# A softmax moved to ScalarE head by head, in a kernel of chunked attention and two MLPs

## The chip, the cores and the metric

The kernel runs on one core of one Trainium2 chip. The metric is the device time of one execution in microseconds. TensorE does the matmuls and some transposes, ScalarE activations and copies, VectorE elementwise work, reductions and 32x32 transposes. SyncE's queue issues nearly all DMAs.

## The reference

Three stages follow one another: attention in chunks, a first pair of layers with an ELU between them, and a second pair with a scaled square of a ReLU.

```python
B, H, S, D = 4, 8, 768, 64;  n_mem = 8;  chunk, left, right = 32, 16, 8
for each chunk c of 32 queries:
    keys = the 8 memory keys, then those from c_start-16 to c_end+8, cut at 0 and S
    scores = q_c @ keys.T / sqrt(D)
    a = exp(scores - max(scores));  a = a / (sum(a) + 1e-9)
    out_c = a @ values
x = out of all heads, as (3072, 512)
h = x @ w_in;   g = where(h > 0, h, exp(min(h, 0)) - 1);  x = g @ w_out      # (512, 2048), (2048, 512)
h = x @ w_in2;  g = s * max(h, 0)**2 + b;                 out = g @ w_out2
```

Every chunk has 64 keys (8 + 16 + 32 + 8); in the first chunk of a batch the 16 to its left don't exist, in the last the 8 to its right. Their scores are masked.

## The kernel before

Attention is cut into 24 units of 128 queries (four chunks) with all 8 heads, six units for each batch; `j` is a unit's place in its batch. A unit goes through three steps. S (`scores`, L213, and `softmax`, L223): 64 small matmuls put the scores of a unit into two PSUM banks, one for each half of the heads, 4 heads of 64 columns in each; then comes the softmax of 8 heads of 64 columns in 128 rows: a mask is added (only in units whose `j` is 0 or 5), the maximum of each head is reduced and subtracted, one ACTIVATE takes the exponential of the whole block, and VectorE sums each head, adds 1e-9, takes the reciprocal and multiplies. P (`step_P`, L245): the block is transposed, for units 0 to 5 on TensorE with a copy to `pt` by `hi_copy` (L174), for later ones by 16 VectorE transposes (L258). V (`values`, L270, and `to_x`, L282): 64 small matmuls with the values, and copies out. From unit 6 on the V step of a unit and the S step of the next share their PSUM tile (`step_VS`, L315).

The tile for scores, of two banks, has one buffer (`ps_a`), so the scores of a unit wait until the softmax of the unit before has read its own for the last time.

The order: units 0, 1 and 2 are worked off before the first h matmul, with the scores of units 3 and 4 (the loop at L506), beside the conversion of the first weights (`split_w`: two ScalarE steps, L131 and L132, two VectorE steps, L135 and L138, a ScalarE copy, L149, and a VectorE subtraction, L184). Then the first layer pair runs in chunks of 128 hidden features for 8 tiles of 384 tokens. Each chunk has 12 matmuls for h (`h1`, L346), a chain of ScalarE and VectorE for the ELU and its split into two parts (L350, L351, L352, L180, L184), and 12 matmuls into four accumulators (`out1`, L386), which come two chunks later. Six chunks of tile 0, all of tile 1, the rest of tile 0 and tiles 2 to 4 have steps of the remaining units between them (`beside`, L512); tiles 0 and 1 also convert weights. From tile 5 on the second pair's weights are prepared. The second pair (`first_layer`, `second_layer`) has seven products for each block; its last copies (L734 on VectorE, L736 on ScalarE) take the two accumulators of the last product, and `put` (L688) stores each with one DMA on SyncE's queue.

The framework's planner orders the instructions of each engine by priority, dependence and its own estimate of durations. On the chip each engine then works off its queue in that order. Loads of k, q, v and weights are all in SyncE's one queue, in order; k, q and v have two buffers, so the load of `v` for a unit waits for the values matmuls of the unit two before it.

Of the kernel before, what the change touches and what calls it, by code (L numbers as in the profile page):

```python
# [8 lines left out]
F32 = mybir.dt.float32  # L9
# [3 lines left out]
AF = mybir.ActivationFunctionType  # L13
ALU = mybir.AluOpType
AX = mybir.AxisListType
# [3 lines left out]
B, H, S, D, NMEM = 4, 8, 768, 64, 8  # L19
CH, LEFT, RIGHT = 32, 16, 8  # L20
# [3 lines left out]
U = 4 * CH  # L24
NKEY = LEFT + U + RIGHT + NMEM
UPB = S // U
NU = B * UPB
NP = H // 2
NU0 = 6
# [4 lines left out]
HN, NT2 = 512, 3  # L34
# [3 lines left out]
NC, NCK = U // CH, LEFT + CH + RIGHT + NMEM  # L38
# [15 lines left out]
def tile_attention_then_two_mlps(ctx, tc, q_in, k_in, v_in, w1, w2, s_in, b_in, out):  # L54
# [17 lines left out]
    nc = tc.nc  # L72
    SCALE = 1.0 / float(D) ** 0.5
    NEG = -1.0e30
# [14 lines left out]
    const = ctx.enter_context(tc.tile_pool(name="const", bufs=1))  # L89
# [19 lines left out]
    part_dram = dp.tile([P, KT, MAXN], F32, name="part1")  # L109

    ident = const.tile([P, P], F32, name="ident")
    cmasks = [const.tile([U, NCK], F32, name=f"cmask{i}") for i in range(2)]
    s_sb = const.tile([P, 1], F32, name="s_sb")
    b_sb = const.tile([P, 1], F32, name="b_sb")

# [46 lines left out]
    op = [actx.enter_context(tc.tile_pool(name="op", bufs=3))]  # L162
# [20 lines left out]
    def sub(lo, src, hi):  # L183
        return nc.vector.tensor_tensor(out=lo, in0=src, in1=f(hi), op=ALU.subtract)  # L184
# [12 lines left out]

    def set_up():

        for m in cmasks:  # L200
            nc.vector.memset(m, 0.0)
        nc.vector.memset(cmasks[0][:CH, NMEM:NMEM + LEFT], NEG)
        nc.vector.memset(cmasks[1][U - CH:, NCK - RIGHT:], NEG)
        make_identity(nc, ident)

    def own_keys(u):

        return sms[u % 2].rearrange("p r z n -> p z r n")

    def by_halves(a):  # L210
        return a.rearrange("p (z r) -> p z r", z=2).unsqueeze(3).to_broadcast([U, 2, NP, NCK])
# [11 lines left out]
    def softmax(u, ps):  # L223
        src = ps[:, :, :NP * NCK].rearrange("p z (r n) -> p z r n", r=NP)
        sm, j = own_keys(u), u % UPB
        if j in (0, UPB - 1):
            mask = cmasks[j > 0].unsqueeze(1).unsqueeze(1).to_broadcast([U, 2, NP, NCK])
            nc.vector.tensor_tensor(out=sm, in0=src, in1=mask, op=ALU.add)
            src = sm
        nmx, sums, rs = (ap2.tile([U, H], F32, tag=nm, name=nm) for nm in ("nmx", "sums", "rs"))  # L230
        nc.vector.tensor_reduce(out=nmx.rearrange("p (z r) -> p z r", z=2), in_=src, op=ALU.max, axis=AX.X)
        nc.vector.tensor_tensor(out=sm, in0=src, in1=by_halves(nmx), op=ALU.subtract)
        nc.scalar.activation(out=sm, in_=sm, func=AF.Exp, scale=SCALE)
        nc.vector.tensor_reduce(out=sums.rearrange("p (z r) -> p z r", z=2), in_=sm, op=ALU.add, axis=AX.X)
        nc.vector.tensor_scalar(out=rs, in0=sums, scalar1=1e-9, scalar2=None, op0=ALU.add)
        nc.vector.reciprocal(out=rs, in_=rs)
        nc.vector.tensor_tensor(out=sm, in0=sm, in1=by_halves(rs), op=ALU.mult)

    def step_S(u):

        ps = two_banks("S")
        scores(u, ps)
        softmax(u, ps)
# [71 lines left out]
    def step_VS(u):  # L315

        ps = two_banks("VS")
        values(u, ps)
        last = scores(u + 1, ps)
        to_x(u, ps, last)  # L320
        softmax(u + 1, ps)


    def mm3(o, a, b, sa, sb, first, last, again=False):

        nc.tensor.matmul(o, sa(a[0]), sb(b[0]), start=first, stop=False, skip_group_check=again)  # L326
        nc.tensor.matmul(o, sa(a[0]), sb(b[1]), start=False, stop=False, skip_group_check=again)  # L327
        return nc.tensor.matmul(o, sa(a[1]), sb(b[0]), start=False, stop=last, skip_group_check=again)  # L328
# [133 lines left out]

    warm(6, pt.rearrange("p h n -> p (h n)")[:, :2 * U])
    set_up()

    nload = [1, 0]
# [67 lines left out]
    def next_piece(layer, i, j):  # L534

        load_pieces(used[0] + 11)
        assert pieces[used[0]] == (layer, i, j)
        used[0] += 1
        return ws[used[0] - 1]
# [102 lines left out]
    def bank(nm):  # L642
        return psp.tile([P, HN], F32, tag="b", name=nm)

    def add(o, x, y):
        return nc.vector.tensor_tensor(out=o, in0=x, in1=y, op=ALU.add)

    def sub2(o, x, y):
        return nc.vector.tensor_tensor(out=o, in0=x, in1=y, op=ALU.subtract)

    def aside(ps, nm):
        o = evp.tile([P, HN], F32, tag="ev", name=nm)
        nc.scalar.activation(out=o, in_=ps, func=AF.Copy)  # L653
        return o
# [30 lines left out]
            sub2(g[:, 1], g[:, 2], g[:, 1])  # L685
            add(g[:, 1], g[:, 1], g[:, 0])

    def put(o, t, m, z):  # L688
        t0 = (2 * t + z) * HN
        nc.sync.dma_start(out=out[:, m, t0:t0 + HN], in_=o)  # L690

    def second_layer(t, gs, beside):

        keep, acc = {}, {}
        for j in ORDER:
            block = {1: 0, 2: 3, 6: 1, 5: 1, 7: 0, 3: 2, 4: 3}[j]
            if j in (1, 2, 5):
                acc[j] = [bank("psL") for _ in range(2)]
            o = acc[BANK[j]]
            for q, g in enumerate(gs):  # L700
                gh, gl = (ghp.tile([P, 2, HN], F32R, tag=nm, name=nm) for nm in ("g2h", "g2l"))
                nc.scalar.activation(out=gh, in_=g[:, block], func=AF.Copy)  # L702
                sub(gl, g[:, block], gh)
                if j == 1:
                    sub2(g[:, 0], g[:, 1], g[:, 0])
                elif j == 2:
                    sub2(g[:, 3], g[:, 3], g[:, 1])
                elif j == 6:
                    sub2(g[:, 1], g[:, 2], g[:, 1])
                for ii in range(2):  # L710
                    w = next_piece(1, 2 * q + ii, j)
                    for m in range(2):
                        mm3(o[m], (w[:, 0], w[:, 1]), (gh[:, ii], gl[:, ii]), lambda a: a[:, m * P:(m + 1) * P],
                            lambda a: a, j in (1, 2, 5) and q == ii == 0, q == 3 and ii == 1,
                            j not in (1, 2, 5))
                if j in (5, 7, 3):
                    next(beside, None)
            for m in range(2):
                if j in (1, 6, 5):
                    keep[j, m] = aside(o[m], "keep")  # L720
                    continue
                r = outp.tile([P, HN], F32, tag="r", name="r")
                if j == 2:
                    add(r, keep[1, m], o[m])
                    put(r, t, m, 0)
                elif j == 7:
                    add(r, keep[5, m], o[m])
                    put(r, t, 2 + m, 1)
                elif j == 3:
                    add(r, keep[6, m], o[m])  # L730
                    put(r, t, m, 1)
                else:
                    if m:
                        nc.vector.tensor_copy(r, o[m])  # L734
                    else:
                        nc.scalar.activation(out=r, in_=o[m], func=AF.Copy)  # L736
                    put(r, t, 2 + m, 0)

    assert next(p2["blocks"], None) is None
    for t in range(NT2):  # L740
        gs = [g2p.tile([P, 4, 2, HN], F32, tag="g", name="g2") for _ in range(NF // 4)]
        for i in range(NF // 2):
            first_layer(t, i, gs[i // 2])
        steps2 = load_blocks(t + 1) if t + 1 < NT2 else iter(())
        second_layer(t, gs, steps2)
        assert next(steps2, None) is None
# [55 lines left out]
```

## Time and profile before

| what | us |
|---|---|
| median of 3 runs | 1099.0 (1098.36 to 1099.37) |
| the profiled execution | 1097.48 |
| its span, first to last instruction | 1095.7 |
| TensorE busy | 1076.3 |
| VectorE busy | 783.9 |
| ScalarE busy | 591.9 |

A busy time is a sum over instructions, with matmuls pipelined. The granted clock is the share of TensorE's full 2.4 GHz that the throttle let through; over the span it is 0.992.

### The profile page before, as it was taken

The numbers are of one execution on the slowest core, as the hardware profiler recorded it, in microseconds if no ns is written. First come the engines' busy times: TensorE is split into PE (matmuls) and PEld (weight loads), VectorE is DVE, ScalarE is ACT, GpSimd is POOL, SyncE is SP. The second block draws the span as 40 slices with busy tenths as digits, with TensorE's granted clock in tenths as the row PEclk, the third lists the DMA queues.
The fourth block names the chain that finished last, engine by engine and source line by source line (L and its number), as shares of the span: only waits on it lengthen the run. The fifth ranks groups of instructions, "written<-read, shape, count | busy, mean of one in ns | idle before, by whom it ended". The sixth has DMA issues, their size and how long they took to land.

```text
span 1095.7 us, 20629 instructions
## 1 busy us (share of the span) xinstructions
PE 1076.3 (98%) x8206; PEld 964.4 (88%) x8206; DVE 783.9 (72%) x1299; ACT 591.9 (54%) x939; POOL 0.7 (0%) x6
## 2 busy tenths in 40 slices
PE   7999999999999999999999999999999999999998
PEld 5889999999999999999999987788888788888886
DVE  6899856777777777898884656796266695375844
ACT  4888534344344346887875455644355653355542
POOL 0000000000000000000000000000000000000000
PEclk7999999999999999999999999999999999999999
DMA  8965032442433316888876366777767777776773
GB/s 305 377 223 214 1 109 94 146 144 93 142 117 121 114 40 206 328 329 303 328 289 253 90 192 190 240 211 224 229 192 196 222 207 226 207 193 192 205 190 124
DMA packets 98113, 213.70 MB, mean 195 GB/s; under 512 B 9952, under 2 KB 27360, under 8 KB 95968
## 3 DMA queue, kind: packets, MB, share of 16 engines
q1 hardware_dynamic: 97440, 211.59, 60.3%
q8 instruction: 65, 1.06, 0.4%
q10 hardware_dynamic: 576, 0.79, 0.2%
q14 instruction: 32, 0.26, 0.1%
HBM read 164.89 MB, written 47.45 MB: 194 GB/s over the span
## 4 chain that ended last, share of the span: by engine, by line
PE 87%; DVE 6%; DMA 4%; ACT 3%; issue 1%; SPq 0%; ACTq 0%; DVEq 0%
PE psH L326 14%; PE psH L328 14%; PE psH L327 14%; PE psL L327 7%; PE psL L328 7%; PE acc L326 7%; PE psL L326 7%; PE acc L327 7%; PE acc L328 7%; DVE pt L258 2%; DMA xc<-y_dram 1%; PE psVS L278 1%; DMA xl<-x_dram 1%; PE psVS L219 1%; PE psV L278 1%
## 5 line engine op out<-in xcount | busy, mean ns | idle before, releaser
L326 PE MATMUL psH<-xh,w 128*128 128x384 f32 x512 | 174.9, 342 | 2.4 <-ACT pt L180 1.0
L326 PE MATMUL acc<-gh,w 128*128 128x384 f32 x512 | 172.7, 338 | 1.3 <-DVE big L380 0.8
L328 PE MATMUL psH<-xh,w 128*128 128x384 f32 x512 | 173.0, 338 | 0.0
L327 PE MATMUL psH<-xl,w 128*128 128x384 f32 x512 | 172.6, 337 | 0.2 <-DVE xl L184 0.2
L328 PE MATMUL acc<-gh,w 128*128 128x384 f32 x512 | 171.8, 336 | 0.0
L327 PE MATMUL acc<-gl,w 128*128 128x384 f32 x512 | 171.7, 335 | 0.0
L702 ACT ACTIVATE g2h<-g 128x1024 fp32r<-128x1024 f32 x84 | 88.9, 1058 | 95.6 <-PE psL L328 95.5
L327 PE MATMUL psL<-g2l,ws 128*128 128x512 f32 x336 | 133.0, 396 | 1.4 <-DVE g2l L184 1.4
L184 DVE TENSOR_TENSOR g2l<-g,g2h 128x1024 fp32r<-128x1024 f32 x84 | 102.3, 1222 | 44.3 <-ACT g2h L702 44.0
L328 PE MATMUL psL<-g2h,ws 128*128 128x512 f32 x336 | 132.9, 395 | 0.0
L326 PE MATMUL psL<-g2h,ws 128*128 128x512 f32 x336 | 132.5, 396 | 0.1
L326 PE MATMUL psH<-xc,ws 128*128 128x512 f32 x336 | 131.7, 397 | 0.5 <-ACT p L653 0.5
L327 PE MATMUL psH<-xc,ws 128*128 128x512 f32 x336 | 131.0, 390 | 0.0
L328 PE MATMUL psH<-xc,ws 128*128 128x512 f32 x336 | 131.0, 390 | 0.0
L350 ACT ACTIVATE g<-psH 128x384 f32<-128x384 f32 x128 | 62.5, 488 | 111.9 <-PE psH L328 65.3
L180 ACT ACTIVATE gh<-g 128x384 fp32r<-128x384 f32 x128 | 67.0, 523 | 88.0 <-DVE g L352 86.9
L352 DVE SCALAR_TENSOR_TENSOR g<-g,psH 128x384 f32<-128x384 f32 x128 | 70.4, 550 | 47.8 <-ACT g L351 46.9
L326 PEld LDWEIGHTS psH<-xh,w 128*128 128x128 f32 x512 | 96.7, 189 | 5.1 <-ACT pt L180 1.2
L326 PEld LDWEIGHTS acc<-gh,w 128*128 128x128 f32 x512 | 96.1, 188 | 2.8 <-DVE big L380 1.1
L327 PEld LDWEIGHTS psH<-xl,w 128*128 128x128 f32 x512 | 96.7, 189 | 0.5 <-DVE xl L184 0.4
L328 PEld LDWEIGHTS psH<-xh,w 128*128 128x128 f32 x512 | 96.7, 189 | 0.2
L327 PEld LDWEIGHTS acc<-gl,w 128*128 128x128 f32 x512 | 96.2, 188 | 0.1
(97 smaller groups left out, 1667.9 us busy)
## 6 DMA issues: line engine op xcount, KB each, us to landing
ws<-s_dram SPq DMA_DIRECT2D x336, 256.0 KB, 3.0
raw<-w SPq DMA_DIRECT2D x64, 512.0 KB, 5.5
s_dram<-right SPq DMA_DIRECT2D x16, 1024.0 KB, 4.6
kb<-k SPq DMA_DIRECT2D x24, 512.0 KB, 5.5
v<-v SPq DMA_DIRECT2D x24, 512.0 KB, 4.1
s_dram<-left SPq DMA_DIRECT2D x16, 768.0 KB, 3.6
q<-q SPq DMA_DIRECT2D x24, 256.0 KB, 5.4
out<-r SPq DMA_DIRECT2D x24, 256.0 KB, 3.5
```

Source lines behind the costliest of these rows:

```text
L180: return nc.scalar.activation(out=hi, in_=src, func=AF.Copy)
L184: return nc.vector.tensor_tensor(out=lo, in0=src, in1=f(hi), op=ALU.subtract)
L219: mm = nc.tensor.matmul(ps[o, z, r * NCK:(r + 1) * NCK], q[rows, r * U + c * CH:r * U + (c + 1) * CH], kb[rows, r, c * NCK:(c + 1) * NCK], ...
L258: nc.vector.transpose(out=pt[k * CH:(k + 1) * CH, :, rows], in_=sm[rows, :, z, n0:n0 + CH])
L278: nc.tensor.matmul(ps[r % 2 * D:(r % 2 + 1) * D, z, o:o + CH], v[rows, (r * NC + c) * D:(r * NC + c + 1) * D], pt[rows, r, cs], start=True ...
L326: nc.tensor.matmul(o, sa(a[0]), sb(b[0]), start=first, stop=False, skip_group_check=again)
L327: nc.tensor.matmul(o, sa(a[0]), sb(b[1]), start=False, stop=False, skip_group_check=again)
L328: return nc.tensor.matmul(o, sa(a[1]), sb(b[0]), start=False, stop=last, skip_group_check=again)
L350: nc.scalar.activation(out=g[:, :n], in_=ps[:, :n], func=AF.Relu, scale=-1.0)
L352: nc.vector.scalar_tensor_tensor(out=g[:, :n], in0=g[:, :n], scalar=-1.0, in1=ps[:, :n], op0=ALU.add, op1=ALU.max)
L702: nc.scalar.activation(out=gh, in_=g[:, block], func=AF.Copy)
```

## The change

The softmax has two forms. Units 3 to 5 keep the old one. All others take the exponential head by head: the maximum is scaled by -1/sqrt(D) and given to ScalarE as a bias, which reads the scores in PSUM, writes the exponentials to SBUF and gives the sum of the head as a second output. For masked units of either form the mask is no longer added: VectorE writes -1e30 over the masked scores in PSUM, and the mask tiles and their four memsets at the start go. The last copy of the program is halved: VectorE copies the left half of the columns and ScalarE the right, and each half has its own store, one on SyncE's queue and one on ScalarE's.

```diff
-    cmasks = [const.tile([U, NCK], F32, name=f"cmask{i}") for i in range(2)]
...
     def set_up():
-        for m in cmasks:
-            nc.vector.memset(m, 0.0)
-        nc.vector.memset(cmasks[0][:CH, NMEM:NMEM + LEFT], NEG)
-        nc.vector.memset(cmasks[1][U - CH:, NCK - RIGHT:], NEG)
         make_identity(nc, ident)
...
     def softmax(u, ps):
         src = ps[:, :, :NP * NCK].rearrange("p z (r n) -> p z r n", r=NP)
         sm, j = own_keys(u), u % UPB
-        if j in (0, UPB - 1):
-            mask = cmasks[j > 0].unsqueeze(1).unsqueeze(1).to_broadcast([U, 2, NP, NCK])
-            nc.vector.tensor_tensor(out=sm, in0=src, in1=mask, op=ALU.add)
-            src = sm
+        if j == 0:
+            nc.vector.memset(src[:CH, :, :, NMEM:NMEM + LEFT], NEG)
+        elif j == UPB - 1:
+            nc.vector.memset(src[U - CH:, :, :, NCK - RIGHT:], NEG)
...
-        nc.vector.tensor_tensor(out=sm, in0=src, in1=by_halves(nmx), op=ALU.subtract)
-        nc.scalar.activation(out=sm, in_=sm, func=AF.Exp, scale=SCALE)
-        nc.vector.tensor_reduce(out=sums.rearrange("p (z r) -> p z r", z=2), in_=sm, op=ALU.add, axis=AX.X)
+        if 3 <= u < NU0:
+            nc.vector.tensor_tensor(out=sm, in0=src, in1=by_halves(nmx), op=ALU.subtract)
+            nc.scalar.activation(out=sm, in_=sm, func=AF.Exp, scale=SCALE)
+            nc.vector.tensor_reduce(out=sums.rearrange("p (z r) -> p z r", z=2), in_=sm, op=ALU.add, axis=AX.X)
+        else:
+            nc.vector.tensor_scalar(out=nmx, in0=nmx, scalar1=-SCALE, scalar2=None, op0=ALU.mult)
+            for h in range(H):
+                z, r = divmod(h, NP)
+                nc.scalar.activation(out=sm[:, z, r], in_=src[:, z, r], func=AF.Exp, scale=SCALE,
+                                     bias=nmx[:, h:h + 1], accum_out=sums[:, h:h + 1])
...
-    def put(o, t, m, z):
+    def put(o, t, m, z, dma=nc.sync, cols=slice(0, HN)):
         t0 = (2 * t + z) * HN
-        nc.sync.dma_start(out=out[:, m, t0:t0 + HN], in_=o)
+        dma.dma_start(out=out[:, m, t0 + cols.start:t0 + cols.stop], in_=o[:, cols])
...
+                    if m and t == NT2 - 1:
+                        a, b = slice(0, HN // 2), slice(HN // 2, HN)
+                        nc.vector.tensor_copy(r[:, a], o[m][:, a])
+                        nc.scalar.activation(out=r[:, b], in_=o[m][:, b], func=AF.Copy)
+                        put(r, t, 2 + m, 0, nc.sync, a)
+                        put(r, t, 2 + m, 0, nc.scalar, b)
+                        continue
```

## Rows read from the trace of the kernel before

**Rows 1.** The page's chain that ended last: shares of the span by engine.
```profile
PE 87%; DVE 6%; DMA 4%; ACT 3%; issue 1%; SPq 0%; ACTq 0%; DVEq 0%
```

**Rows 2.** Windows: stretch, its length, busy us of each engine, PEclk, DMA share, GB/s.
```profile
8.00:16.00 8.00, 4.46 (x140) 3.19 (x140) 7.29 (x16) 3.84 (x7) 0.00 (x0) 0.99 1.00 389
16.00:33.00 17.00, 15.42 (x344) 13.32 (x344) 12.71 (x24) 9.37 (x17) 0.00 (x0) 0.50 0.86 318
...
56.00:64.00 8.00, 7.92 (x100) 6.89 (x99) 7.92 (x17) 6.84 (x15) 0.00 (x0) 1.00 0.93 375
64.00:76.00 12.00, 9.97 (x121) 8.72 (x119) 11.60 (x28) 11.12 (x22) 0.00 (x0) 1.00 0.19 56
...
130.00:390.00 260.00, 257.49 (x3217) 250.63 (x3216) 185.12 (x441) 107.54 (x203) 0.00 (x0) 1.00 0.36 117
```

**Rows 3.** Timeline, 6 to 27 us: start, length, engine, line, what, [idle before <-releaser].
```profile
6.24 0.86 PE L219 MATMUL psS<-kb,q 64*32 64x64 f32 x64
7.14 0.69 DVE L228 TENSOR_TENSOR sm<-psS,cmask 128x512 f32<-128x512 f32 x1 [5.42 <-PE psS L219]
8.92 0.86 PE L219 MATMUL psS<-kb,q 64*32 64x64 f32 x64
10.13 0.61 ACT L233 ACTIVATE sm<-sm 128x512 f32<-128x512 f32 x1
13.94 0.69 DVE L237 TENSOR_TENSOR sm<-sm,rs 128x512 f32<-128x512 f32 x1
15.15 0.68 ACT L131 ACTIVATE raw<-raw 128x512 f32<-128x512 f32 x1 [0.40 <-DMA raw<-w]
16.28 0.57 ACT L180 ACTIVATE pt<-psP 128x512 f32<-128x512 f32 x1
16.91 1.93 PE L278 MATMUL psV<-pt,v 64*64 64x32 f32 x64 [0.20 <-ACT pt L180]
22.79 1.11 PE L251 MATMUL psP<-ident,sm 128*128 128x128 f32 x4
24.65 1.72 PE L278 MATMUL psV<-pt,v 64*64 64x32 f32 x56 [0.75 <-ACT pt L180]
```

**Rows 4.** Waits of SyncE's queue, 0 to 40 us: total us, times, longest.
```profile
SPq L175 <- PE psV L278: 15.3, 4, 6.7
```

**Rows 5.** ScalarE's groups by shape: busy us, mean ns of one, idle before.
```profile
L702 ACT ACTIVATE g2h<-g 128x1024 fp32r<-128x1024 f32 x84 | 88.9, 1058 | 95.6 <-PE psL L328 95.5
L683 ACT ACTIVATE g<-g,b_sb,s_sb 128x2048 f32<-128x2048 f32 x24 | 50.4, 2099 | 2.1 <-DVE g L680 1.5
L420 ACT ACTIVATE left<-t 128x256 fp32r<-128x256 f32 x7 | 2.9, 414 | 0.5 <-DVE t L138 0.5
```

**Rows 6.** Timeline of ScalarE, two conversions with no wait between them.
```profile
40.48 0.69 ACT L131 ACTIVATE raw<-raw 128x512 f32<-128x512 f32 x1
41.03 0.73 ACT L132 ACTIVATE raw<-raw 128x512 int32<-128x512 uint32 x1
```

**Rows 7.** VectorE's groups by shape, columns as in rows 5.
```profile
L234 DVE TENSOR_REDUCE sums<-sm 128x8 f32<-128x512 f32 x24 | 16.4, 684 | 9.9 <-ACT sm L233 9.7
L236 DVE RECIPROCAL rs<-rs 128x8 f32<-128x8 f32 x24 | 4.8, 200 | 0.5
L455 DVE MEMSET pt<- 128x512 f32 x1 | 0.5, 485 | 0.9 <-PEq L785 0.9
```

**Rows 8.** Timeline of VectorE: the mask of unit 6.
```profile
56.15 0.68 DVE L228 TENSOR_TENSOR sm<-psS,cmask 128x512 f32<-128x512 f32 x1
```

**Rows 9.** Timeline, 219 to 225 us: a later unit's last transposes, its values.
```profile
219.79 1.28 DVE L258 STREAM_TRANSPOSE pt<-sm 32x128 f32<-32x128 f32 x4
...
223.31 1.14 PE L278 MATMUL psVS<-pt,v 64*64 64x32 f32 x64
```

**Rows 10.** The end: the last copy in the timeline; the last stores (issue to landing).
```profile
1092.01 0.69 DVE L734 COPY r<-psL 128x512 f32<-128x512 f32 x1 [6.08 <-PE psL L328]
...
out<-r SPq DMA_DIRECT2D x2, 256.0 KB, 2.0
```

## The prediction

> **What bounds the kernel now.** The shares of the chain that ended last come first [rows 1]: TensorE holds 87% of it, so an edit on ScalarE or VectorE is worth something only where TensorE waits. The windows by stage say where that is [rows 2]. In the long stage in which 15 of the later units run beside the first layer pair, TensorE is busy 257.49 of 260 us. Early on it isn't: 4.46 of 8 us from 8 to 16, 15.42 of 17 from 16 to 33, but that at a granted clock of 0.50, the 1.2 GHz level, and 9.97 of 12 from 64 to 76, where VectorE (11.60) and ScalarE (11.12) are the full ones. So there are three places to look at: the attention of units 0 to 2 ahead of the first h matmul, the stretch up to 76 us with the softmax of units 5 and 6, and the tail after the last matmul.
>
> The timeline of the first 25 us has the chain [rows 3]. Scores of unit 0 end at 7.10; mask, maximum and subtraction take three VectorE instructions of 0.69; the exponential starts only at 10.13; the product that ends the softmax runs from 13.94 to 14.63; the copy of the transpose starts at 16.28, behind two weight conversions on ScalarE's queue, of which the one at 15.15 waited for its DMA; the values matmuls of units 0 and 2 start at 16.91 and 24.65. SyncE's queue hangs on them too: it stands 15.3 us at loads of v until the values of an earlier unit are done [rows 4].
>
> **Part by part, first the prices.** No ACTIVATE of 64 columns with a bias column and a sum is in the trace. Those without per-partition operands take 1058 ns for 1024 columns and 414 for 256 [rows 5]: 0.84 ns a column and 200 fixed. The one with two such operands takes 2099 for 2048 [rows 5]; less 1715 for its columns and 200 this leaves 184, or 92 for one. A head alone is then 54 + 200 + 92 = 346 ns. In a row of ready ones the next starts early, 0.55 after one of 0.69 [rows 6], so 0.21 us a head. That is the low end, with the sum for nothing. The high end adds for each sum a tiny operation at the 200 ns of VectorE's on 8 columns [rows 7], and some overlap lost: 0.43. I take 0.28, nearer to the low end, because what the rows show of one column more at an ACTIVATE (92 ns) is far less than an instruction. Eight heads: 2.24 us (1.7 to 3.4). The memset into PSUM has at most 128 columns; one of 512 takes 485 ns [rows 7], so about 0.17, between a quarter of that and all of it. Scaling the maximum is one more operation on 8 columns, 0.2.
>
> In exchange a unit loses a sum of 0.68 and a subtraction, priced like the mask's addition at 0.69, on VectorE, and an exponential of 0.61 on ScalarE [rows 3, 7]. A unit with j of 0 or 5 also trades the mask's addition for the memset.
>
> **Units 0 to 2.** The change adds a wait: the scores' two banks, one buffer, are now read until the last head, where before the subtraction (in unit 0 the mask) was the last to read them. What is queued behind that on TensorE is the next unit's scores. Unit 0: scores end at 7.10, memset, maximum and scaling by 8.25, heads by 10.5; scores of unit 1 not before 10.55, now 8.92. One turn is scores 0.86, maximum 0.69, scaling 0.2, heads 2.24 and 0.15 of handing over: 4.15. Heads of unit 1 end at 14.65, of unit 2 at 18.8, or at 20.4 with three conversions of the first weights between them (0.55 each from start to start [rows 6]). Two operations of 0.2 and the product follow, 1.25 alone, 2.65 with two weight steps of 0.69 between them, so unit 2 is normalised at 20.05 to 23.1. Transposes (1.11) and copy (0.57) in rows 3 bring its values to 21.75 to 24.8, in the middle 23.3. From the other side, TensorE's order keeps 24.65 - 16.91 = 7.7 us between the values of units 0 and 2; unit 0 can be transposed and copied by 14.6, so not before 22.3. I take 22.85, 1.8 us earlier than now, and the first h matmul moves with it, as SyncE's queue is let go earlier too. At 0.21 a head it is the floor of 22.3, a gain of 2.3; at 0.43 the heads of unit 2 end 3.6 us later and the values come at about 26.9, a loss of 2.3. Heads over some 0.35 us lose here.
>
> **Units 5 and 6.** Unit 6's mask is added at 56.15, where VectorE is full [rows 2, 8]; unit 5 comes ahead of it. Unit 5 keeps its old exponential but trades the mask for a memset: 0.5 us less. Unit 6, masked and on the new path, relieves VectorE of 0.69 + 0.69 + 0.68 for 0.37: 1.7. ScalarE gets 2.24 for 0.61, 1.6 more, and has 8 - 6.84 = 1.16 free in 56 to 64 [rows 2]. In 64 to 76, 2.03 us of TensorE are lost while VectorE's queue is full. Between a gain of 2.0 (that idle time) and a loss of 0.5 (ScalarE's overflow) I take a gain of 0.7, VectorE being the fuller of the two. At 0.43 a head the overflow is 1.7.
>
> **Units 7 to 23.** ScalarE gets 1.6 us with each, 24 for the 15 units of a stage in which it is busy 107.54 of 260 us; VectorE, at 185.12, loses 1.2 with each [rows 2]. No engine fills up. From scores to product an unmasked chain loses 0.69 + 0.61 + 0.68 and gets 0.2 + 2.24, 0.5 more, and at 0.43 a head 1.7 more; between the end of a unit's last transposes (219.79 + 1.28) and its values at 223.31 there are 2.2 us [rows 9]. That is the cover, so nothing; the ends are -2.5, all that TensorE is idle in this stage [rows 2], and 1, with the cover gone in a unit or two. A relu that queues behind eight heads is at most 2.24 us late, which the order of the code covers: its chunk's second matmuls come two chunks later.
>
> **The start.** The four memsets of the masks lie in the 5.42 us in which VectorE waits for the first scores [rows 3]: nothing either way.
>
> **The tail.** The last copy is 0.69 from 1092.01, its store 2.0 from issue to landing [rows 10]. A half has 256 columns, which takes 0.41 in rows 5 on ScalarE; I use it for both engines. If both halves run at once the copy is 0.28 shorter and each store moves half: a gain of 0.5 at most. One after the other they take 0.85 with the handing over, 0.16 later, and the smaller store may give that back: no gain. Nothing else stands in ScalarE's queue by then. I take 0.2. The Trainium skill, PSUM — Partial Sum Buffer (PSUM bank collisions raise a hardware error), says that two engines must not touch one bank in the same partitions at once, even at different columns and even to read. The halves lie in one bank, so by that rule they go one after the other, and the sum would be 0.2 us higher; no run here shows such a pair.
>
> **Sum.** -1.8 - 0.7 + 0 - 0.2 = -2.7 on the profiled execution's 1097.48 (the span of 1095.7 and 1.8 around it): 1094.8. The runs' median is 1.5 above that execution, so 1096.3.
>
> **The rivals.**
> *The clock stays up* (1092.3). It is at 0.99 from 8 to 16, where TensorE is busy 4.46 of 8 us, and 0.50 from 16 to 33 [rows 2], so it falls after the sparsest stretch. A unit's values take 1.93 us at the low level and 1.14 at the high one [rows 3, 9]. If the fall doesn't come, three values save 2.4 and the first h matmuls, transposes and scores, which fill the rest of these 17 us, up to half of what they take; I count 4 in all, as ScalarE and the DMAs are in that chain too: 1096.3 - 4. For it: scores, warming matmuls, transposes and values of units 0 and 1 lie closer together between 10.5 and 16. Against it: TensorE does less between 8 and 10.5, and the fall may come earlier. The Trainium skill, TensorE: Matmul & The Clock Gate (Part 1: The HAM clock gate), has the low clock as the default that activity lifts; these rows look like that.
> *The heads cost 0.43* (1102.8), the slower side. The sum is an operation of its own, and from 0.35 a head on units 0 to 2 lose: +2.3 there, +1.7 at unit 6, -0.2 in the tail, 3.8 on 1099.0. For it: an operation on 8 columns still takes 0.2 [rows 7], so little ones are all fixed cost. Against it: ScalarE's instructions overlap.
> *The gain is hidden* (1098.7). The copy of unit 0's transpose stood behind a conversion that waited for a DMA until 15.15 [rows 3]. If it stays there, unit 0's values start at 16.9 as now, and the tail's 0.2 and 0.1 of unit 6 are left. For it: ScalarE's queue is in order and that DMA doesn't move. Against it: the planner has eight heads to place and will order anew.
>
> **How the numbers follow.** Forecast 0.47, with its own range of 1094.5 to 1098.5; the clock 0.18; dear heads 0.15; hidden 0.20. 0.2% of this time is 2.2 us, about what a measurement of this kernel can tell from no change: faster is under 1096.8. The forecast's range gives 0.29 faster and 0.18 same; the clock 0.18 faster; dear heads 0.13 slower and 0.02 same; hidden 0.02, 0.15 and 0.03. Together 0.49, 0.35 and 0.16. The range goes from below the clock's case to near that of the dear heads, 1091.5 to 1102.
>
> **What would show it.** Right: heads 0.25 to 0.32 us apart; scores of unit 1 at about 10.5; values of unit 2 before 23.5; TensorE idle under 2 us in the stretch that is now 64 to 76; the stage from 130 to 390 as full as now. Wrong: heads 0.35 or more apart, scores that hold the values up, a clock that falls before 15 us, or new waits beside units 7 to 23.

## The result: 0.5% slower, and the profile after

The changed kernel takes 1104.7 us (median of 12 runs, 1100.6 to 1108.4) against 1099.1 for the kernel before, beside it on the same chip: a ratio of 1.0052, 95% interval 1.0034 to 1.0070, so 3.7 to 7.7 us slower. The forecast was 1096.3 with a range up to 1102.0. The profiled execution took 1107.3 us with a span of 1105.4; it lies 2.6 us above its median, and that of before 1.5 below its own. Below, a ratio is given in us of 1099. It can differ from the quotient of two medians, by up to 1.4 us here.

The page's chain that ended last, shares of the span by engine, answers to [rows 1]: TensorE's share has fallen from 87%, while VectorE's and ScalarE's have risen.

```profile
PE 84%; DVE 7%; ACT 4%; DMA 4%; issue 1%; SPq 0%; DVEq 0%; ACTq 0%
```

The windows of the changed kernel, columns as in [rows 2]:

```profile
8.00:16.00 8.00, 4.47 (x90) 3.11 (x88) 3.79 (x9) 5.79 (x21) 0.00 (x0) 0.84 0.94 340
16.00:33.00 17.00, 12.26 (x395) 10.39 (x392) 12.43 (x26) 13.88 (x49) 0.00 (x0) 0.50 0.85 291
56.00:64.00 8.00, 7.96 (x105) 7.31 (x104) 7.91 (x18) 7.49 (x27) 0.00 (x0) 1.00 0.98 363
64.00:76.00 12.00, 10.46 (x103) 9.72 (x103) 11.58 (x28) 10.60 (x22) 0.00 (x0) 1.00 0.54 208
130.00:390.00 260.00, 254.09 (x3098) 244.72 (x3097) 165.01 (x427) 130.84 (x420) 0.00 (x0) 0.99 0.37 118
```

Two stretches are worse. From 16 to 33 us TensorE is busy 12.26 us instead of 15.42. In the long stage from 130 to 390 us it is busy 254.09 instead of 257.49, although VectorE has 20 us less to do there and ScalarE 23 us more, neither near full.

The timeline of the first 30 us of the changed kernel answers to [rows 3]:

```profile
6.76 0.86 PE L214 MATMUL psS<-kb,q 64*32 64x64 f32 x64
7.71 0.17 DVE L222 MEMSET psS<- 32x128 f32 x1 [6.31 <-PE psS L214]
8.88 1.28 ACT L235 ACT_TABLE_LOAD   x1 [8.88 <-DVE nmx L232]
10.18 0.31 ACT L235 ACTIVATE sm<-psS,nmx 128x64 f32<-128x64 f32 x1
10.39 0.19 ACT L235 ACTIVATION_READ_ACCUMULATOR sm<-psS,nmx 128x1 f32 x1
10.48 0.30 ACT L235 ACTIVATE sm<-psS,nmx 128x64 f32<-128x64 f32 x1
...
12.71 0.89 PE L214 MATMUL psS<-kb,q 64*32 64x64 f32 x64 [2.39 <-ACT sm L235]
...
15.74 1.93 PE L280 MATMUL psV<-pt,v 64*64 64x32 f32 x64 [0.69 <-ACT pt L179]
...
16.65 0.31 ACT L235 ACTIVATE sm<-psS,nmx 128x64 f32<-128x64 f32 x1
...
19.17 1.19 PE L214 MATMUL psS<-kb,q 64*32 64x64 f32 x64 [1.50 <-ACT sm L235]
...
28.91 1.93 PE L280 MATMUL psV<-pt,v 64*64 64x32 f32 x64 [1.49 <-ACT pt L179]
```

The heads are 0.29 us apart. The table load now stands behind the wait for the first maximum: it starts at 8.88 us, where before it started at 0.73. Scores of units 1 and 2 start at 12.71 and 19.17, held by the heads of the unit before, and the values of unit 2 at 28.91 instead of 24.65. The waits of TensorE up to 31 us name the same two:

```profile
PE psS L214 <- ACT sm L235: 4.9, 3, 2.4
PE psV L280 <- ACT pt L179: 2.9, 3, 1.5
```

ScalarE's groups by shape (columns as in [rows 5]) show that the sum is an instruction of its own; in the timeline above the next ACTIVATE starts inside it:

```profile
L235 ACT ACTIVATE sm<-psVS,nmx 128x64 f32<-128x64 f32 x136 | 40.5, 323 | 16.1 <-DVE nmx L232 16.1
L235 ACT ACTIVATION_READ_ACCUMULATOR sm<-psVS,nmx 128x1 f32 x136 | 29.4, 216 | 0.0
```

**Where the loss builds up.** To follow it, take in both traces the moments at which TensorE goes over from the h matmuls to those of the accumulators and back, of which there are 257 in each, and subtract the n-th of before from the n-th of after. The first h matmul is 3.6 us late. At the 97 us of before that is gone (-2.1, of which an estimated 1.7, from the lengths of their pieces before, is the scores of unit 7, not yet done). Between 141 and 155 us the lag goes from -1.4 to +2.3, at 168 us by 3.3 more, at 256 by 1.7, at 308 by 1.5, and it is 9.9 from 355 on. After that the two kernels run alike. So the whole loss is made beside units 7 to 23, where the prediction had put zero. These 9.9 us are those of two executions, one above its median and one below; between the medians it is 5.6.

### The profile page after: what moved, and what is told of

The parts are those of the page before. It is cut to its first block, busy times and chain, and to the rows that moved or that the text cites. A ratio compares the mean times of both kernels' runs of the same rounds, so it can differ in the third digit from the quotient of the medians.

```text
span 1105.4 us, 20933 instructions
## 1 busy us (share of the span) xinstructions
PE 1080.8 (98%) x8206; PEld 968.1 (88%) x8206; DVE 755.6 (68%) x1274; ACT 629.0 (57%) x1255; POOL 0.7 (0%) x6
## 4 chain that ended last, share of the span: by engine, by line
PE 84%; DVE 7%; ACT 4%; DMA 4%; issue 1%; SPq 0%; DVEq 0%; ACTq 0%
PE psH L328 14%; PE psH L329 13%; PE psH L330 13%; PE psL L329 7%; PE psL L330 7%; PE psL L328 7%; PE acc L328 7%; PE acc L330 7%; PE acc L329 6%; DVE pt L260 2%; PE psVS L280 1%; ACT sm L235 1%; DMA xc<-y_dram 1%; DMA xl<-x_dram 1%; PE psVS L214 1%
## 5 line engine op out<-in xcount | busy, mean ns | idle before, releaser
L328 PE MATMUL acc<-gh,w 128*128 128x384 f32 x512 | 173.3, 339 | 1.9 <-DVE big L382 1.0
L329 PE MATMUL psH<-xl,w 128*128 128x384 f32 x512 | 173.5, 339 | 0.0
```

## The experiments

All were timed beside the kernel before. Intervals are of 95%. All but two (the one that only moves scores and the one with an unused tile) have the halved copy at the end.

**One: is it the heads at all, and in which units?** Three kernels from the changed one differ in one condition, the units that keep the old softmax. The masks stay written into PSUM. The planner gives each of the three its own order on TensorE, so a difference between two of them holds one of order too.

```diff
-        if 3 <= u < NU0:
+        if u >= 0:         # e1: old softmax in all units
+        if u >= 3:         # e2: heads in units 0 to 2 alone
+        if u < NU0:        # e3: heads from unit 6 on alone
```

> The changed kernel with the old softmax (subtract, one exponential, sum on VectorE) in all units; the masks overwritten in PSUM and the halved last copy stay. Theory P (price): a head is an ACTIVATE and a read of the accumulator, 0.29 us together, with a table load of 1.28 that now waits for the first maximum; that made the first h matmuls 2.6 us late and the values of later units wait 4.0 us for transposes. P expects both gone: first relu at 33 us as before, values waiting about 1 us from 130 to 400, 1098 to 1099.5. Theory O (order): the planner's new order of TensorE costs, above all the values of unit 7, which stand in pieces of 2 and 6 between single matmuls of the accumulators (pieces also in this kernel's order, 5 of them). O expects about 2.5 us of the loss to stay: 1101 to 1102.

Measured: 1100.5 us, ratio 1.0030 [1.0018, 1.0043]: +3.3 us with no head in it.

> Heads one by one in units 0 to 2 alone. P: first relu 2.6 us late as in the changed kernel, but no more waits of values than before from 130 to 400: 1100 to 1102. A third theory, W: what is lost before the first h matmul is caught up in the stretch up to 80 us, where VectorE is full and has less to do, so that units 0 to 2 cost nothing in the end: 1098 to 1100. O: 1101 to 1102 as in the run with the old softmax everywhere, since its order has the same pieces.

Measured: 1100.0 us, ratio 1.0014 [1.0003, 1.0024]. Against e1 it is 1.8 us less, but the two intervals overlap and the orders differ, so a gain from the heads of units 0 to 2 is not shown.

> Heads one by one in units 6 to 23 alone. P: first relu at 33 us as before, values waiting 3 to 4 us for transposes from 130 to 400, 1101 to 1104. W: the loss is in these units, 1104 to 1105, as large as the changed kernel's. O: its order has more pieces (75 switches in the first 1800 matmuls, 69 in the changed kernel, 65 before), so the loss is at least the changed kernel's.

Measured: 1106.6 us, ratio 1.0077 [1.0065, 1.0089]: +8.5 us. The later heads, with the order that comes with them, cost some 5 us on top of e1. (In its profile the granted clock also stands at 0.50 for 6.8 us from 60.9 on, which no other one has.)

So the loss has two parts: one that comes with the later heads, and one that comes without any. For the second the timeline of TensorE has a candidate. In the kernel before, the scores of unit 7 are done by 91 us, laid in pieces between h matmuls, and its values run in one block at 151 us:

```profile
90.40 0.34 PE L219 MATMUL psVS<-kb,q 64*32 64x64 f32 x14
...
151.37 1.14 PE L278 MATMUL psVS<-pt,v 64*64 64x32 f32 x64
152.43 0.86 PE L219 MATMUL psVS<-kb,q 64*32 64x64 f32 x64
```

In the changed kernel the planner has put 62 of these 64 scores at 141.59 (46 of them at 142.69 in e1), so the softmax and the transposes come late and the values go in pieces between single accumulator matmuls:

```profile
141.59 0.84 PE L214 MATMUL psVS<-kb,q 64*32 64x64 f32 x62
...
150.97 0.32 PE L280 MATMUL psVS<-pt,v 64*64 64x32 f32 x8
152.06 0.30 PE L280 MATMUL psVS<-pt,v 64*64 64x32 f32 x2 [0.40 <-DVE pt L260]
152.83 0.31 PE L280 MATMUL psVS<-pt,v 64*64 64x32 f32 x6
...
155.79 0.78 PE L280 MATMUL psVS<-pt,v 64*64 64x32 f32 x38
156.50 0.86 PE L214 MATMUL psVS<-kb,q 64*32 64x64 f32 x64
```

What took 1.92 us from 151.37 to 153.29 before now stretches over 6.4 us.

**Two: would it help to hold the values together?** In the changed kernel the first values matmul of each unit from 6 on waits for the unit's last transpose, so that no values run in pieces.

```diff
+                LAST[u] = nc.vector.transpose(out=pt[...], in_=sm[...])
...
+                        if u in LAST:
+                            wait(mm, LAST.pop(u))
```

> The changed kernel, with the first values matmul of each unit from 6 on made to wait for the last of its 16 transposes, so that the planner keeps the values in one block (no pieces in the order). O: the broken block near 150 us goes and with it 2.5 us: 1101.5 to 1102.5. P: the accumulator reads still lengthen the chain from scores to transposes, 1104 to 1106.

Measured: 1105.8 us, ratio 1.0072 [1.0057, 1.0086]. No help: unit 7's values are one block again, but it starts only at 154.89, after a wait of 1.88 us for the transposes. The pieces are a sign of transposes that end late, not the disease.

**Three: the late scores alone.** The kernel before with one dependence more: the last two score matmuls of unit 7 wait for the h matmuls of the chunk at 145 us. (They are four in the trace, which has two rows for each of the program's small matmuls: the 64 of a unit are 32 in the program.) Nothing else in TensorE's order changes but the values of unit 7, which go in pieces again.

```diff
+        held = u == NU0 + 1
...
+                    if held and (r, c, z) == (NP - 1, NC - 1, 0):
+                        wait(mm, HM[-1])
```

> The kernel before, with one dependence more: the last scores of unit 7 wait until the planner has placed the first h matmuls of tile 0 that come after all of tile 1. Nothing else differs in TensorE's order but the place of these scores and, following from it, that the values of unit 7 stand in pieces between single accumulator matmuls, as in the run with heads in units 0 to 2. Theory O, now sharper: the masks and the new softmax close holes in the planner's plan, the scores of unit 7 come 50 us later, and values of unit 7 and all after it are late. O expects a loss of 2 to 3.5 us: 1100.5 to 1102. Rival: the place of these scores is harmless and the mask overwritten in PSUM itself costs the 3 us of the run with the old softmax everywhere; then no loss here, 1098 to 1099.

Measured: 1101.7 us, ratio 1.0033 [1.0017, 1.0049]: +3.6 us, as much as e1. Its lag goes from 2.3 to 5.4 us between 141 and 155 us. So where the planner puts the scores of unit 7 is worth 3.6 us (1.9 to 5.4), enough for all of e1; that e1's loss is this one is argued from the like size and the like rows. In the profiled execution, 5.5 us above the median, the lag goes on from 5.4 to 8.9 at 355 us, beside the units behind, with the clock up. The memsets in units 0, 5 and 6 and the missing mask tiles are what e1 has early in the program, so one or several of these make the planner move them (the later masks and the halved copy are not: the next kernel has them, and its scores of unit 7 stay); which one was not separated.

**Four: the later heads alone.** The kernel before with the new softmax (heads and memset) from unit 8 on; TensorE's instructions stand in the same order as before. A second kernel leaves out the sum as a second output and lets VectorE sum as before; TensorE's order is again the same.

```diff
-        nc.vector.tensor_tensor(out=sm, in0=src, in1=by_halves(nmx), op=ALU.subtract)
...
+        if u < 8:
+            nc.vector.tensor_tensor(out=sm, in0=src, in1=by_halves(nmx), op=ALU.subtract)
...
+        else:
+            nc.vector.tensor_scalar(out=nmx, in0=nmx, scalar1=-SCALE, scalar2=None, op0=ALU.mult)
+            for h in range(H):
...
```

> Units 0 to 7 as before, masks and all; heads one by one and masks in PSUM from unit 8 on; halved last copy. TensorE's order is the one of the kernel before, matmul for matmul. Theory P (price of the heads, 2.3 us of ScalarE in front of the relu of a chunk): values wait 3 to 4 us for transposes from 130 to 430 and the granted clock falls once or twice: 1101 to 1103. Theory O: all loss of the later units comes from the order, so none here: 1098 to 1099.

Measured: 1103.4 us, ratio 1.0036 [1.0021, 1.0051]: +4.0 us.

> As the run with heads from unit 8 on, but without the second output: the sums are one reduction on VectorE again. TensorE's order is the one of the kernel before. If the reads of the accumulator are what makes the later units late, ScalarE has 0.2 us a head less and half of that run's loss goes, 1099.5 to 1101, although VectorE gets 0.68 more a unit. If it is that ScalarE holds the relu of the next chunk up for eight instructions, about the same loss stays; if VectorE is what counts, more than that run's loss.

Measured: 1100.9 us, ratio 1.0022 [1.0008, 1.0037]: +2.4 us. The sum's share, 1.6 us, is good to about 1.5. What the sum costs on ScalarE is clear, though. In this kernel the eight heads of unit 8 take 1.75 us, and the heads of all sixteen units are 0.20 us apart:

```profile
154.51 1.75 ACT L244 ACTIVATE sm<-psVS,nmx 128x64 f32<-128x64 f32 x8 [0.97 <-DVE nmx L241]
```

With the sum they are 0.29 apart. Its instruction of 0.22 us thus costs 0.09 us a head, 0.7 a unit.

**Five: which of the later units pay?** In the trace of before the time between the end of a unit's last transpose and its first values matmul is not the same for all. For unit 15 it is 3.5 us; for unit 13 it is 0.2 us. The rows of before for these two, unit 13's last three transposes ahead of its values, and for unit 15 its last eight:

```profile
253.38 0.96 DVE L258 STREAM_TRANSPOSE pt<-sm 32x128 f32<-32x128 f32 x3
254.53 1.14 PE L278 MATMUL psVS<-pt,v 64*64 64x32 f32 x64
...
281.76 2.58 DVE L258 STREAM_TRANSPOSE pt<-sm 32x128 f32<-32x128 f32 x8
...
287.83 1.14 PE L278 MATMUL psVS<-pt,v 64*64 64x32 f32 x64
```

Read so for all units, 8, 10, 13, 16, 18 and 19 have -1.7 to 0.8 us there (below nothing, because the values of the first heads start while the last are transposed), and units 9, 11, 12, 14, 15, 17, 20, 21 and 22 have 1.4 us or more; unit 23, the last, was put with these. Two kernels split the sixteen:

```diff
-        if u < 8:
+        if u not in (8, 10, 13, 16, 18, 19):                       # uncovered
+        if u not in (9, 11, 12, 14, 15, 17, 20, 21, 22, 23):       # covered
```

> The kernel before with the heads (and the mask as a memset) only in units 8, 10, 13, 16, 18 and 19, the copy at the end halved, TensorE's instructions in the same order as before. In the trace of before the first values matmul of these six starts -1.7 to 0.8 us after the unit's last transpose ends, so nothing covers a longer softmax there. Theory (the loss of the later units sits where there is no cover): +3 to +4 us, nearly all of the +4.0 of heads in all units from 8 on, with waits of the values for pt of 2 us or more in the attention stage. Rival (each unit with heads costs the same, through ScalarE's queue and the relus behind it): 6 of 16 units, +1.5 us.

Measured: 1103.1 us, ratio 1.0024 [1.0005, 1.0043]: +2.6 us.

> The same with the heads only in the other ten, units 9, 11, 12, 14, 15, 17 and 20 to 23, whose values start 1.4 to 14 us after the last transpose in the trace of before. Theory (cover): within 1 us of before, steps of the drift only at units without heads, if any. Rival (the same for each unit): 10 of 16, +2.5 us.

Measured: 1098.9 us, ratio 0.9994 [0.9981, 1.0007]: -0.7 us, so at most 0.8 us slower. Ten units with heads cost nothing that shows, six cost 2.6 us of the 4.0 that sixteen do, and these two intervals overlap. The 2.6 alone would fit the rival too; it is the ten that refute it, and the two kernels, beside each other, differ by 3.5 us, good to 2.0. The waits of TensorE from 130 to 430 us go with it. Before, then the heads in the uncovered units, then in the covered ones:

```profile
PE psVS L278 <- DVE pt L258: 1.1, 3, 0.5
```

```profile
PE psVS L289 <- DVE pt L269: 3.2, 6, 1.0
```

```profile
PE psVS L289 <- DVE pt L269: 0.6, 2, 0.4
```

Most of what this execution lost (1105.2 us) is at two of the six. What one such unit costs shows at unit 13, whose rows of before stand above. With heads in the uncovered units TensorE's timeline has its values in three pieces, behind two waits:

```profile
256.20 0.59 PE L289 MATMUL psVS<-pt,v 64*64 64x32 f32 x24
257.13 0.30 PE L289 MATMUL psVS<-pt,v 64*64 64x32 f32 x2 [0.34 <-DVE pt L269]
258.38 0.78 PE L289 MATMUL psVS<-pt,v 64*64 64x32 f32 x38 [0.95 <-DVE pt L269]
```

and the windows of that kernel show what follows:

```profile
256.00:260.00 4.00, 2.71 (x130) 2.10 (x128) 2.76 (x9) 1.87 (x4) 0.00 (x0) 0.95 0.00 0
260.00:264.00 4.00, 4.00 (x19) 3.99 (x16) 1.93 (x3) 0.81 (x2) 0.00 (x0) 0.62 0.95 307
```

TensorE is idle for 1.3 us, and then the granted clock falls to 0.50, the lower level of 1.2 GHz, for 3.4 us from 259.6 on: the mean is 0.62 over the next four microseconds. Its lag grows by 2.0 us at the values and by 1.4 more behind them, and the same pair comes at unit 16 (0.8 and 1.2). The changed kernel has it at units 8 and 16; here are the windows at unit 8:

```profile
165.00:170.00 5.00, 4.09 (x123) 3.18 (x125) 4.14 (x14) 1.47 (x3) 0.00 (x0) 1.00 0.01 2
170.00:175.00 5.00, 5.00 (x49) 4.91 (x42) 1.80 (x6) 3.60 (x19) 0.00 (x0) 0.66 0.87 277
```

In the trace of before the clock stays up through the whole stage [rows 2], and so it does with the heads in the covered units. But it also stays up in the profile of heads from unit 8 on (1101.8 us), whose lag grows by 1.5 us at unit 13 from the waits alone. So the fall comes in some executions only.

The longer softmax is not all of it at unit 13. The stretch from the end of its scores to the end of its last transpose takes 14.8 us with the heads in the uncovered units, against 12.4 before, but 1.55 of these 2.3 pass ahead of its maximum, which starts 2.90 us after the scores instead of 1.35: the planner, which kept TensorE's order, now has another chunk's ELU steps ahead of it on VectorE, and on ScalarE ahead of the copy of the unit before. In the other five this stretch is between 0.5 us shorter and 0.6 longer.

**Six: is the start worth anything?** The kernel before with heads in units 0 to 2, an exponential of one column ahead that loads the table early, and a second score tile for units 1 and 3, so that their scores need not wait for the heads before.

```diff
+    ps_s = vctx.enter_context(tc.tile_pool(name="ps_s", bufs=1, space=PSUM))
...
+        ps = ps_s.tile([P, 2, 512], F32, tag="a", name="psS2") if u in (1, 3) else two_banks("S")
...
+    tab = const.tile([P, 1], F32, name="tab")
+    nc.scalar.activation(out=tab, in_=pt[:, 0, :1], func=AF.Exp)
```

> Heads one by one in units 0 to 2 alone, the old masks from unit 3 on, the table loaded early by an exponential of one column, a second score tile of two banks in the first stage for units 1 and 3, and the halved last copy. From the first h matmul on TensorE's order is the one of the kernel before. The wait for the score banks (5.3 us in the run with heads in units 0 to 2) and the table load of 1.28 behind the first maximum are gone. By the price of a head (0.29) the values of unit 2 come at about 23 us instead of 28.9, 1.5 ahead of the kernel before: 1096 to 1097.5. If the stretch up to 80 us absorbs what is gained before it, as it caught up what was lost: 1098 to 1099. If ScalarE's queue is what holds the values up: 1099 to 1101.

Measured: 1090.7 us, ratio 0.9933 [0.9912, 0.9953]: 7.4 us faster than before. But the first h matmul is only 1.4 us earlier, and at the end of the first pair the trace is not ahead at all (+0.7 at 419 us). The gain comes in the second pair, where each of the 1008 matmuls into psL follows the one before after 0.2267 us instead of 0.2333, 6.7 us in all. Nothing in these matmuls was changed. What was is where their operands lie: the one-column tile takes 32 bytes of each partition, and every tile behind it moves by as much. g2h goes from byte 93376, a multiple of 64, to 93408, which is one of 32 only; the weights in ws stay where they were. Two kernels take this apart: the kernel before with an unused tile of 32 bytes, and the kernel above with 64 bytes for its tile. (The addresses are those that the program gives its tiles.)

```diff
+    pad = const.tile([P, 8], F32, name="pad")          # before, never used
...
-    tab = const.tile([P, 1], F32, name="tab")
+    tab = const.tile([P, 16], F32, name="tab")         # two tiles
```

> The kernel before with one more tile of 32 bytes per partition in the constants' pool, never used: every instruction is the same, and all tiles of the second layer pair's own pools lie 32 bytes further on (g2h from 93376 to 93408, no longer a multiple of 64). Theory (the -7.4 us of the kernel with heads in units 0 to 2 and a second score tile came from this shift, since its one tiny tile makes the same, and the 1008 matmuls into psL there followed each other every 0.2267 us against 0.2333 in every other trace): -6.7 us, 0.2267 between psL matmuls. Rival (the gain came from the start): no change, 0.2333.

Measured: 1092.1 us, ratio 0.9926 [0.9910, 0.9942]: 8.1 us faster, with every instruction as before.

> The kernel with heads in units 0 to 2, old masks elsewhere, an early table load and a second score tile, its tiny tile made 64 bytes long, so that the second pair's tiles lie 64 bytes further on than before instead of 32. Theory (shift): the gain of 7.4 us falls to 0 to 1.5 us, psL matmuls every 0.2333 us again; what is left is what the earlier start is worth at the end. Rival (the start itself): still -6 to -8 us.

Measured: 1098.3 us, ratio 0.9996 [0.9983, 1.0009]: the gain is gone. TensorE's groups for these matmuls (busy us, mean ns of one; they overlap) show it, before, before with 32 bytes, and two tiles with 64:

```profile
L327 PE MATMUL psL<-g2l,ws 128*128 128x512 f32 x336 | 133.0, 396 | 1.4 <-DVE g2l L184 1.4
```

```profile
L328 PE MATMUL psL<-g2l,ws 128*128 128x512 f32 x336 | 131.0, 390 | 1.4 <-DVE g2l L185 1.4
```

```profile
L339 PE MATMUL psL<-g2l,ws 128*128 128x512 f32 x336 | 132.9, 396 | 1.3 <-DVE g2l L185 1.3
```

So the shift is shown. But the kernel with 64 bytes is no clean measure of the start: the 384-column matmuls of its first pair follow each other every 175.0 ns from 430 to 615 us, against 173.7 before and 173.3 with 32 bytes, and over all 3072 of them that is some 3 us. The clean pair is the kernel with two tiles and 32 bytes beside the unused tile of 32 bytes, with the same addresses: 7.4 and 8.1 us below before, each good to some 2 us. So no gain from heads in units 0 to 2, even freed from the wait for the score tile, is shown. The unused tile is one of the two fastest kernels here, and owes nothing to the change; the mask tiles that the change takes away move the same addresses by 512 bytes, a multiple of 64, and the psL matmuls of the changed kernel keep 0.2333.

## Why the prediction was wrong

The step that failed is the one under units 7 to 23: "That is the cover, so nothing". It took the 2.2 us of one unit [rows 9] as the cover of all. In six of the units there is 0.8 us or less, and heads in these six alone cost 2.6 us; in all units from 8 on 4.0. The 0.5 us that the step has a chain grow by was about right (0.2 to 1.0 in the ten covered units), but at unit 13 it grew by 2.3, most of that by the planner's order on VectorE and ScalarE. The bound that the same step named for the cover gone, 1 us, was too small as well: at unit 13 alone the waits cost 1.5 to 2.0 us, and in some executions the clock that fell behind them 1.4 more.

What no step had: the planner's order. "The planner has eight heads to place and will order anew" stood there as an argument for one rival at the start, but the price of an order was never put into the range. Moved scores of unit 7 cost 3.6 us. With 4.0 for the later heads that makes 7.6, against 5.7 measured. The -1.8 between e1 and e2 would bring it to 5.8, but each of these is good to some 1.5 us and the -1.8 is not shown to be the heads', so the close sum is partly luck.

The other steps:
- **The price of a head**: 0.29 us, predicted 0.28, and 0.20 without the sum, predicted 0.21. The reason for the difference was wrong: the rival of dear heads was right that the sum is an instruction of its own (216 ns), but it starts 0.2 us into its ACTIVATE and the next ACTIVATE starts 0.09 us behind it, so only these 0.09 show. That rival's time, 1102.8, was nearer than the forecast; its mechanism did not happen.
- **Units 0 to 2**: predicted 1.8 us earlier, found 4.3 us later (28.91 against 24.65). A turn takes 6.46 us, not 4.15. The table load of 1.28 us (at 0.73 us before) now comes after the first maximum, and the heads of unit 1 start only at 16.65: its scores end at 13.57, but VectorE takes the maximum at 14.42 and scales it at 15.62, behind the product of unit 0 and weight steps, and ScalarE does two conversions first; "heads of unit 1 end at 14.65" took both engines as free. The Trainium skill, ScalarE: Activation LUTs (What ACT_TABLE_LOAD costs), gives about 1283 ns for the load, and the trace agrees (1283). By 97 us the late start is caught up, so it is not in the result. An early one did not last either: with two score tiles TensorE is 1.7 us ahead at 76 us and 0.1 at 97, behind a clock that fell to 0.50 at 74.8.
- **The clock stays up**: it did not. It falls to 0.50 at 13.4 us for 20.5 us (before: at 15.8 for 17.1; the mean from 8 to 16 is 0.84, was 0.99), after TensorE's idle time of 2.39 us ahead of the scores of unit 1, as the prediction had named for a sign against it.
- **Units 5 and 6**: TensorE loses 1.54 us from 64 to 76, where it lost 2.03, but the scores of unit 7 have left this stretch, so the gain of 0.7 is neither shown nor ruled out.
- **The start**: the memset is 0.17 us as estimated. That it is nothing for the time holds for its duration; e1, whose order moved with no head in it, shows that it may have a price through the order.
- **The tail**: predicted 0.2, found about 0.1 (from the start of the last matmul to the end of the span 4.0 us, before 4.1). The halves went one after the other, ScalarE's with a wait for VectorE's:

```profile
1101.84 0.42 DVE L737 COPY r<-psL 128x256 f32<-128x256 f32 x1 [6.08 <-PE psL L330]
1102.30 0.38 ACT L738 ACTIVATE r<-psL 128x256 f32<-128x256 f32 x1 [0.56 <-DVE r L737]
```

The Trainium skill, PSUM — Partial Sum Buffer (PSUM bank collisions raise a hardware error), does not let two engines into the same partitions of one bank at once, and this program keeps to it; the rows agree with the case that the prediction had weighed by that rule.

Open is which of the planner's inputs moves the scores of unit 7, how the 4.0 us divide between the longer softmax and the planner's order on VectorE and ScalarE, and how much of them is the sum's own instruction.

## What to carry to other kernels

A cover read at one instance of a repeated step is not the cover of all: read it for every instance, and price a longer chain at those that have none, with the clock that may fall behind the wait. Where a planner orders the program, an edit to one step can move another; compare the engines' orders before and after before asking what the edited instructions cost. And when a variant wins, look for where in the span the gain lies: here 7 us of a "better start" were an address.

## What the runs showed of the hardware

- Matmuls of 512 columns with the moving operand at a multiple of 64 bytes (g2h at 93376, 92864 or 93440) follow each other every 0.2333 us; at an odd multiple of 32 (93408) every 0.2267. The matmuls of the second pair into psH, whose operand lies at 172000, an odd multiple of 32 too, follow each other every 0.228 in all these kernels, close to the fast ones into psL. The weights' tile ws has the same address in all, at an odd multiple of 32.
- The weights' address counts too. In the first pair of the kernel with 64 bytes the moving operands of 384 columns all lie at multiples of 128 bytes; with weights at multiples of 128 the matmuls follow each other every 173.5 ns, with weights at odd multiples of 32 every 176.3. The same two sets of chunks are 174.0 and 173.5 apart in the kernel before, whose moving operands lie at odd multiples of 64, so it is not the chunks. Which pairs of addresses are slow, beyond those that ran here, is open.
- Behind a unit's values that came in pieces with waits between them, the granted clock fell to 0.50 for 3.4 us at a time, and TensorE's lag grew by 1.2 to 1.5 us under it where the waits can be told apart from it (at 313.8 us in the changed kernel, 259.6 and 310.8 with heads in the uncovered units). Behind the values of unit 6, near 75 us, it fell so in nine of the twelve profiles of experiments, that of the unused tile among them (76.5), whose instructions are those of before; the profiled execution of before had no such fall there. Each such fall cost 1.3 to 1.6 us of lag where TensorE's order is that of before from the first h matmul to there, so one profile can be that much luckier than another; whether this is why the profiled execution of before took 1097.5 beside a median of 1099.0 is not shown.
- The sum of an ACTIVATE over 64 columns is an ACTIVATION_READ_ACCUMULATOR of 190 to 270 ns, overlapped by the next ACTIVATE: such heads are 0.29 us apart with it and 0.20 without.
